# The first eight loads of a one-core gated-mix kernel: who issues them, in what order, and how many warming matmuls stand ahead of them

## The chip, the cores and the metric

The kernel runs on 1 core of one Trainium2 chip. The metric is device time in microseconds of one execution; lower is better. The kernel before took 150.2 us (median of 3 runs, 149.66 to 150.45). A profile is one further execution; its own time and the span of its records are given below.

## What is computed

`x` has 2048 rows of 512 features, all in bf16. Two branches read it and a gate mixes them:

```python
g = sigmoid((x * gate_w).sum(-1))                 # one number per row
# branch a: linear attention with 32 heads of 16 features
q, k, v = split(x @ wqkv)
pq, pk  = q @ w_phi, k @ w_phi                    # per head
phi_q   = concat(softmax(pq), softmax(-pq));  phi_k likewise
kv, z   = sum_s phi_k v,  sum_s phi_k
a = (phi_q kv) / (phi_q z + 1e-6) @ wo
# branch b
b = relu(x @ w1) @ w2                             # w1 is 512 x 1376
out = g * a + (1 - g) * b
```

## The kernel before, in words

Every step is a named task of one engine. Tasks are put down with `add(name, engine, function, deps)`; the table `ORDER` (line 17) fixes by hand in which order each engine runs its tasks, and `settle` (line 133) turns the dependences into semaphore waits in front of a task, leaving out those that another wait already implies. So the order of the work is wholly static: SP issues its DMAs one after the other in the order of `ORDER["sp"]`, ScalarE (ACT) issues its DMAs and its activations in the order of `ORDER["act"]`, and so on. `dur`, `lat` and `boost` are numbers for a planner that is no longer run; they change nothing.

The rows of `x` are taken in four chunks of 512. The matmuls need `x` transposed (`XT`). Chunks 1 to 3 are transposed by DMA (`x1`, `x2`, `x3`). Chunk 0 is wanted first, so it is loaded as it is, in four tiles of 128 rows x 512 features (128 KB each: `x00` to `x03`, issued through `load`, line 306), into a part of `FT` that is free at the start, and TensorE transposes it against an identity matrix.

The front of the kernel, which is all that the change touches, runs like this:

- POOL builds index tiles (`iota_r`, `iota_i`, `iota_c`), then runs two memsets: `ones` (line 283, a column of ones in `VS`) and `hpad`. VectorE (DVE) builds the identity `IDN` (task `ident`, line 354).
- TensorE (PE) first runs `warm0`: six matmuls of 128x512 on a constant, whose result nobody reads (`WARM`, line 218; line 292). They need nothing but the constant.
- Eight loads of 128 KB bring the four tiles of `x` and the first 512 columns of the four row blocks of W1 (`w1a0` to `w1a3`). SP issues `x00 w1a0 w1a2 x02 x03`; ACT issues `x01 w1a1 w1a3`. Behind them SP goes on with `w1b`, `wphi`, `wkT` (a transposing DMA, line 311), `w1c`, `wv` and then `x1`, which waits for `w1c`.
- PE then runs, in this order: `xt00 xt01 xt10 xt11` (two transposing matmuls each, line 384, tiles 0 and 1 of `x`), `hh00 hh01` (four matmuls each, line 439, W1's row block 0 times row tile 0 and row tile 1), `hh1` and `hh2` (four matmuls of 256 columns each, row blocks 1 and 2), `xt20 xt21`, `hh3`, `xt30 xt31`, `hh4` (row block 3), then `hr0 hr1` (line 445) and the rest of the first hidden blocks.
- The transposed tiles leave PSUM by a ScalarE copy (`xe00`, `xe10`, ...; line 396) and a DVE copy (`xe01`, ...; line 399). `hh00` waits for `xe00` and `w1a0`; `hh01` for `xe10`; `hh1` for `w1a1`, `hh2` for `w1a2`, `hh3` for `w1a3`.
- ScalarE's first activation is `xe00`. Its function table has to be loaded before it; that instruction is put ahead of the first activation, behind the three DMAs in ACT's order.

Everything that follows (the hidden layer `h*` at line 425, projections `pr_*` at line 545, `v*` at line 526, the feature maps on ScalarE, DVE and POOL, `kv*`, `nd*`, and the two output matmul groups `b*` at line 676 and `a*` at line 682) is left as it is by the change.

Of the kernel before, what the change touches and what calls it, by code (L numbers as in the profile page):

```python
# [5 lines left out]
ACT = mybir.ActivationFunctionType  # L6
# [9 lines left out]

ORDER = {
# [4 lines left out]
    ),  # L22
# [5 lines left out]
    ),  # L28
    "act": (
# [153 lines left out]
def bass_gated_mix__linear_kernel_hedgehog__dense_activation_relu__prompt_kernel(  # L183
# [11 lines left out]
    x2 = A_x.rearrange("b s d -> (b s) d")  # L195
# [4 lines left out]
    P = 128  # L200
# [14 lines left out]
    NPH, NOM, NOT, NOS = 7, 3, 4, 5  # L215
    NDB, AB = (6, 7), (3, 4, 5, 2)
    GATE_LIMIT = 40.0
    WARM = (6 * (512,),)
    RL = 400.0
    FE = "dve"  # L220

    with ExitStack() as es:
        E = es.enter_context

        def sb(name, shape, dt):
            return E(nc.sbuf_tensor(name, shape, dt))
# [6 lines left out]
        W1 = sb("W1", [P, ND, W1C], BF16)  # L233
# [30 lines left out]
        EP = sb("EP", [P, NT], FP32)  # L264
# [11 lines left out]
        add = g.add  # L276
# [10 lines left out]
        one = nc.const_aps.tensor(1.0, (P, 1), BF16).tensor  # L287
        ones_w, ones_m = (bass.AP(tensor=one, offset=0, ap=[[1, P], [0, n]]) for n in (P, 512))

        def pe_warm(q, cols):  # L290
            for n in cols:
                last = q.matmul(PS[:, 2, 0:n], ones_w, ones_m[:, 0:n], start=True, stop=True)  # L292
            return last

        for n, cols in enumerate(WARM):
            add(f"warm{n}", "pe", lambda q, c=cols: pe_warm(q, c), (), dur=sum(cols) / 1200.0, boost=3000.0)
# [3 lines left out]
        def after_last(name, eng):  # L300
            if eng in queue:
                g.follow(queue[eng], name)
            queue[eng] = name

        def load(name, eng, out_, in_, deps=(), dur=0.1, lat=6.0, **how):
            add(name, eng, lambda q: q.dma_start(out=out_, in_=in_, **how), deps, dur=dur, lat=lat, dma=True,
                boost=1e4)
            after_last(name, eng)
# [9 lines left out]
        w1r = B_w1.rearrange("(j p) n -> p j n", p=P)  # L318
        x0r = x2[chunk(0), :].rearrange("(m p) d -> p m d", p=P)
        wvr = A_wqkv[:, 2 * D:3 * D].rearrange("(j p) n -> p j n", p=P)  # L320
        def load_x(m, eng, lat):
            load(f"x0{m}", eng, XN[:, m, :], x0r[:, m, :], dur=0.45, lat=lat)

        def load_w(j, eng, lat):
            load(f"w1a{j}", eng, W1[:, j, 0:512], w1r[:, j, 0:512], dur=0.45, lat=lat)

        load_x(0, "sp", 2.95)
        load_x(1, "act", 3.1)
        load_w(0, "sp", 3.2)
        load_w(1, "act", 3.4)  # L330
        load_w(2, "sp", 3.8)
        load_w(3, "act", 3.95)
        load_x(2, "sp", 4.0)
        load_x(3, "sp", 3.9)
# [141 lines left out]
        for n, (kind, a, k) in enumerate(units):  # L476
            b = GB4[n] if n < 4 else FB[2] if n == 4 else HB[(n - 4) % len(HB)]
            if kind == "h":
                halved = n < 4
                deps = [*xof[a], *w1of[k], prev, *freed[b]]  # L480
                if k == KT - 1:
# [18 lines left out]
                    deps, dur=(0.22 if k < 2 else 0.44) if halved else 0.87,  # L500
# [5 lines left out]
            else:  # L506
                deps = ["wqT", *wbd, prev, *freed[b]]
# [22 lines left out]
        for m in range(NT):  # L530
            def add(*a, boost=20.0 * (len(widths) * 2 - m // 2 - VLAG), **how):
                return g.add(*a, boost=boost, **how)
# [17 lines left out]
        for jn, (kind, tiles) in enumerate(jobs):  # L550
# [66 lines left out]
            else:  # L617
# [4 lines left out]
                    dur=0.11 + 0.207 * w)  # L622
# [24 lines left out]
                for m in tiles:  # L647
# [39 lines left out]
                    if m == NT - 1:  # L687
# [4 lines left out]
                        for h2 in range(2):  # L692
# [25 lines left out]
                            else:  # L718
                                add(f"oe{m}_1", "dve", lambda q, m=m, b=b, cs=cs: q.tensor_scalar(  # L719
                                    OSB[:, m % NOS, cs], PS[:, b, 0:cs.stop - cs.start], OMG[:, m:m + 1], None, ALU.mult), need,  # L720
                                    dur=0.4)
                            add(f"st{m}_{h2}", ("act", "sp")[h2], lambda q, m=m, cs=cs: q.dma_start(
                                out=o2[m * P:(m + 1) * P, cs], in_=OSB[:, m % NOS, cs]), (f"oe{m}_{h2}",), dur=0.5,
                                lat=1.5, dma=True)
# [55 lines left out]
```

## Time and profile before

| what | us |
|---|---|
| median of 3 runs (lowest, highest) | 150.2 (149.66, 150.45) |
| the profiled execution's own time | 149.87 |
| its span, from its first record to its last | 148.3 |
| PE busy in the span | 145.5 (98%) |
| DVE / POOL / ACT busy | 111.7 / 109.6 / 91.4 |
| moved by DMA | 16.11 MB, 109 GB/s over the span |

The profiled execution took 1.57 us more than its span shows, so 1.57 us lie outside the records. Times in the views count from the span's start. In a row of the timeline the first number is the start, the second how long the (merged) instructions took, then engine, line, operation, the tile written and the one read, the shape and the count; in brackets stands the idle time before it and what ended it. PEld rows are weight loads, which run beside PE's matmuls. SPq and ACTq rows are DMA issues: the time in them is the issuing, not the transfer. Matmuls are pipelined: each row's duration is longer than the distance to the next matmul, so rates are read from starts.

### The profile page before, as it was taken

How to read it: one execution, taken by the hardware profiler on the slowest of the kernel's cores; microseconds unless marked ns; L12 is line 12 of the kernel's file. 1: busy time of each engine (PE TensorE's matmuls, PEld its weight loads, DVE VectorE, ACT ScalarE, POOL GpSimd, SP SyncE). 2: the span in 40 equal slices, each digit the busy share in tenths (PEclk: the TensorE clock that was granted, in tenths of full speed). 3: DMA queues.
4: the chain of work that ended last, by engine and by line, in shares of the span. 5: the costliest groups of instructions: out<-in, count | busy, mean ns of one | idle time of the engine just before them, and what ended most of it. 6: DMA issues, size and time to landing. Idle time of an engine off the chain costs nothing.

```text
span 148.3 us, 2542 instructions
## 1 busy us (share of the span) xinstructions
PE 145.5 (98%) x1009; PEld 75.3 (51%) x1009; DVE 111.7 (75%) x169; ACT 91.4 (62%) x126; POOL 109.6 (74%) x72
## 2 busy tenths in 40 slices
PE   7999999999999999999999999999999999999994
PEld 2875444445654475445444545455444444445453
DVE  2433666998896948989999997999999988634502
ACT  3475769799969765898983937175583751310141
POOL 4000499999999999999999999999999793150000
PEclk9999999999999999999999999999999999999999
DMA  4998999910040001000000093646957785556752
GB/s 139 324 256 220 169 187 214 340 51 4 0 73 0 0 4 38 0 0 4 0 0 0 7 141 71 141 95 138 183 119 167 180 214 116 141 134 158 64 157 92
DMA packets 46363, 16.11 MB, mean 109 GB/s; under 512 B 39856, under 2 KB 46352, under 8 KB 46352
## 3 DMA queue, kind: packets, MB, share of 16 engines
q1 hardware_dynamic: 43760, 13.61, 42.6%
q10 hardware_dynamic: 2592, 2.34, 4.9%
q8 instruction: 8, 0.13, 0.4%
q14 instruction: 3, 0.02, 0.1%
HBM read 4.41 MB, written 2.10 MB: 44 GB/s over the span
## 4 chain that ended last, share of the span: by engine, by line
PE 98%; DVE 0%; issue 0%
PE PS L676 24%; PE PS L425 21%; PE PS L545 19%; PE PS L526 9%; PE PS L682 9%; PE PS L611 3%; PE PS L654 3%; PE PS L433 2%; PE PS L292 2%; PE PS L698 2%; PE PS L439 2%; PE PS L445 1%; PE PS L408 1%; PE PS L384 1%; PE PS L709 1%; DVE OSB L719 0%
## 5 line engine op out<-in xcount | busy, mean ns | idle before, releaser
L590 POOL TENSOR_TENSOR TS<-PB,MX 128x1024 bf16<-128x1024 bf16 (+1 forms) x18 | 30.9, 1723 | 14.5 <-DVE MX L581 14.5
L676 PE MATMUL PS<-W,HT 128*128 128x512 bf16 (+1 forms) x165 | 38.1, 379 | 0.0
L597 DVE TENSOR_REDUCE ZB<-FT 128x128 f32<-128x2048 bf16 (+1 forms) x18 | 36.6, 2031 | 1.8 <-ACT FT L595 1.8
L595 ACT ACTIVATE FT<-TS 128x2048 bf16<-128x2048 bf16 (+1 forms) x18 | 30.9, 1718 | 9.6 <-POOL TS L590 9.5
L425 PE MATMUL PS<-XT,W 128*128 128x512 bf16 x144 | 34.7, 379 | 0.0
L590 POOL TENSOR_TENSOR TS<-MN,PB 128x1024 bf16<-128x1024 bf16 (+1 forms) x18 | 30.9, 1726 | 0.8 <-DVE MN L583 0.8
L545 PE MATMUL PS<-WP,XT 128*128 128x512 bf16 x128 | 30.6, 379 | 0.0
L604 POOL TENSOR_TENSOR FT<-FT,SC 128x2048 bf16<-128x2048 bf16 (+1 forms) x9 | 29.6, 3293 | 0.0
L503 ACT ACTIVATE HT<-PS 128x512 bf16<-128x512 f32 x40 | 22.6, 597 | 5.4 <-PE PS L425 4.6
L581 DVE TENSOR_REDUCE MX<-PB 128x64 bf16<-128x1024 bf16 (+1 forms) x18 | 19.5, 1085 | 5.9 <-ACT PB L577 5.9
L676 PEld LDWEIGHTS PS<-W,HT 128*128 128x128 bf16 (+1 forms) x165 | 15.4, 98 | 16.9
L730 ACT ACTIVATE OSB<-PS,OMG 128x512 bf16<-128x512 f32 x14 | 9.6, 686 | 21.1 <-PE PS L682 20.5
L583 DVE TENSOR_REDUCE MN<-PB 128x64 bf16<-128x1024 bf16 (+1 forms) x18 | 19.3, 1084 | 3.2 <-ACT PB L577 3.2
L425 PEld LDWEIGHTS PS<-XT,W 128*128 128x128 bf16 x144 | 13.7, 98 | 15.4
L577 ACT ACTIVATE PB<-PS 128x1024 bf16<-128x1024 f32 (+1 forms) x18 | 16.7, 927 | 7.2 <-PE PS L545 4.0
L545 PEld LDWEIGHTS PS<-WP,XT 128*128 128x128 bf16 x128 | 12.1, 98 | 13.5
L526 PE MATMUL PS<-WV,XT 128*128 128x512 bf16 x64 | 16.4, 379 | 0.0
L627 POOL TENSOR_TENSOR FT<-FT,SR 128x1024 bf16<-128x1024 bf16 (+1 forms) x9 | 15.7, 1740 | 0.7
L682 PE MATMUL PS<-WO,OT 128*128 128x512 bf16 x60 | 14.9, 378 | 0.0
L663 DVE SCALAR_TENSOR_TENSOR OTM<-PS,EG,RD 128x256 bf16<-128x256 f32 x32 | 13.8, 463 | 0.2
L661 DVE RECIPROCAL RD<-PS 128x16 f32<-128x16 f32 x32 | 6.4, 232 | 9.0 <-PE PS L654 8.8
L535 ACT ACTIVATE VS<-PS 128x512 bf16<-128x512 f32 x16 | 9.6, 602 | 4.3 <-PE PS L526 4.3
(55 smaller groups left out, 106.6 us busy)
## 6 DMA issues: line engine op xcount, KB each, us to landing
out_dram<-OSB ACTq DMA_DIRECT2D x14, 128.0 KB, 2.2
W<-in_B_w_dram SPq DMA_DIRECT2D x1, 1280.0 KB, 7.5
W<-in_B_w_dram SPq DMA_DIRECT2D x1, 512.0 KB, 4.5
WV<-in_A_wqkv_dram SPq DMA_DIRECT2D x1, 512.0 KB, 4.9
WO<-in_A_wo_dram SPq DMA_DIRECT2D x1, 512.0 KB, 7.5
FT<-in_A_x_dram SPq DMA_DIRECT2D x3, 128.0 KB, 3.1
W<-in_B_w_dram SPq DMA_DIRECT2D x1, 352.0 KB, 4.1
W<-in_B_w_dram ACTq DMA_DIRECT2D x2, 128.0 KB, 3.3
```

Of the source, the lines that this page charges most:

```text
L425: last = q.matmul(PS[:, b, :], W1[:, j, k * P:(k + 1) * P], XT[:, j, chunk(c)], start=(j == 0), stop=(j == ND - 1))
L503: add(f"rl{a}_{k}", "act", lambda q, a=a, k=k, b=b: q.activation(HT[:, k, chunk(a)], PS[:, b, :], ACT.Relu), (prev,), dur=0.6, boost=RL)
L526: last = q.matmul(PS[:, 2, :], XT[:, j, m * P:(m + 1) * P], WV[:, j, :], start=(j == 0), stop=(j == ND - 1))
L545: last = q.matmul(PS[:, n, :], XT[:, j, m * P:(m + 1) * P], WP[:, s, j, :], start=(j == 0), stop=(j == ND - 1))
L581: add(f"mx_{J}", "dve", lambda q, sl=sl, w=w, i=pbg: q.tensor_reduce(MX[:, sl, 0:w * H], i, AX.X, ALU.max), (f"ev_{J}", old("t1")), dur=0. ...
L583: add(f"mn_{J}", "dve", lambda q, sl=sl, w=w, i=pbg: q.tensor_reduce(MN[:, sl, 0:w * H], i, AX.X, ALU.min), (f"ev_{J}", old("t2")), dur=0. ...
L590: add(f"{tn}_{J}", "pool", lambda q, o3=o3, a3=a3, b3=b3: q.tensor_tensor(o3, a3, b3, ALU.subtract), (f"{'mx' if sg == 0 else 'mn'}_{J}", ...
L595: add(f"ex_{J}", "act", lambda q, fs=fs, ts=ts, w=w: q.activation(FT[:, fs, 0:w * F], TS[:, ts, 0:w * F], ACT.Exp), (f"t1_{J}", f"t2_{J}", ...
L597: add(f"sm_{J}", "dve", lambda q, fs=fs, sl=sl, w=w: q.tensor_reduce(ZB[:, sl, 0:2 * w * H], FT[:, fs, 0:w * F].rearrange("p (g d) -> p g ...
L604: add(f"nm_{J}", "pool", lambda q, f3=f3, sl=sl, w=w: q.tensor_tensor(f3, f3, SC[:, sl, 0:2 * w * H].unsqueeze(2).to_broadcast([P, 2 * w * ...
L676: last = q.matmul(PS[:, ab, :], HT[0:r, k, m * P:(m + 1) * P], W2[0:r, k, :], start=(k == 0), stop=False)
L682: last = q.matmul(PS[:, ab, :], OT[:, m % NOT, t, :], WO[:, t, :], start=False, stop=(t == ND - 1))
```

## The change

```diff
 ORDER = {
     "sp": (
-        "x00 w1a0 w1a2 x02 x03 w1b wphi wkT w1c wv x1 x2 wqT x3 gw w2a w2b wo hx0 hx1 hx2 tq0 tq1 "
+        "x00 x01 w1a0 w1a1 x02 x03 w1b wphi wkT w1c wv x1 x2 wqT x3 gw w2a w2b wo hx0 hx1 hx2 tq0 tq1 "
...
     "act": (
-        "x01 w1a1 w1a3 xe00 xe10 xe20 xe30 rl0_0 rl0_1 rl0_3 rl0_2 rl0_4 fe1_1 fe1_3 rl0_5 ev_k0 rl0_8 rl0_6 "
+        "first w1a2 w1a3 xe00 xe10 xe20 xe30 rl0_0 rl0_1 rl0_3 rl0_2 rl0_4 fe1_1 fe1_3 rl0_5 ev_k0 rl0_8 rl0_6 "
...
-    WARM = (6 * (512,),)
+    WARM = (5 * (512,),)
...
-        def load_w(j, eng, lat):
-            load(f"w1a{j}", eng, W1[:, j, 0:512], w1r[:, j, 0:512], dur=0.45, lat=lat)
+        def load_w(j, eng, lat, deps=()):
+            load(f"w1a{j}", eng, W1[:, j, 0:512], w1r[:, j, 0:512], deps, dur=0.45, lat=lat)
 
         load_x(0, "sp", 2.95)
-        load_x(1, "act", 3.1)
+        load_x(1, "sp", 3.1)
         load_w(0, "sp", 3.2)
-        load_w(1, "act", 3.4)
-        load_w(2, "sp", 3.8)
+        load_w(1, "sp", 3.4)
+        add("first", "act", lambda q: q.activation(EP[:, 0:1], bass.AP(tensor=one, offset=0, ap=[[1, P], [1, 1]]), ACT.Copy),
+            (), dur=1.5)
+        after_last("first", "act")
+        load_w(2, "act", 3.8, ("ones",))
         load_w(3, "act", 3.95)
```

SP now issues six of the eight first loads, `x00 x01 w1a0 w1a1 x02 x03`, one more than before. ACT issues two, `w1a2` and `w1a3`, and the first of them waits until POOL's memset `ones` is done. Ahead of both stands a new activation, `first`, which copies one constant per partition into a column of `EP` that is overwritten much later; the function table is now loaded ahead of it. One of the six warming matmuls is taken away. Nothing else moves.

## The prediction

> **What bounds the kernel now.** I read the page first, sections 1 and 4: who is busy, and what the chain that ended last is made of.
>
> ```profile
> span 148.3 us, 2542 instructions
> ...
> PE 145.5 (98%) x1009; PEld 75.3 (51%) x1009; DVE 111.7 (75%) x169; ACT 91.4 (62%) x126; POOL 109.6 (74%) x72
> ...
> PE 98%; DVE 0%; issue 0%
> ```
>
> The chain is PE alone. The waits of PE over the whole span have one row:
>
> ```profile
> PE PS L292 <- PEq L765: 0.8, 1, 0.8
> ```
>
> That is the start, before the first warming matmul. Behind it PE waits for nobody long enough to be listed, so the kernel lasts as long as PE's list of matmuls, counted from when PE can begin it. Only three things can move the end: when the real matmuls begin, how fast they run, and a hole that a late load tears. So the timeline of the first microseconds comes next (shown in part).
>
> ```profile
> 0.74 0.41 ACTq L306 DMA_DIRECT2D FT<-in_A_x_dram  x1
> 0.74 0.40 SPq L306 DMA_DIRECT2D FT<-in_A_x_dram  x1
> ...
> 0.77 2.72 PE L292 MATMUL PS<-const-bfloat16-1.0 128*128 128x512 bf16 x6 [0.77 <-PEq L765]
> ...
> 1.42 0.67 POOL L283 MEMSET VS<- 128x128 bf16 x1
> ...
> 2.15 1.28 ACT L396 ACT_TABLE_LOAD   x1 [2.15 <-issue]
> ...
> 3.55 0.78 PEld L384 LDWEIGHTS PS<-IDN,FT 128*128 128x128 bf16 x8 [0.96 <-issue]
> ...
> 3.58 1.01 PE L384 MATMUL PS<-IDN,FT 128*128 128x128 bf16 x8
> 3.99 0.81 ACT L396 ACTIVATE XT<-PS 128x256 bf16<-128x256 f32 x2 [0.56 <-PE PS L384]
> ...
> 4.43 1.98 PE L439 MATMUL PS<-XT,W 128*128 128x128 bf16 x16
> 6.14 0.32 PEld L384 LDWEIGHTS PS<-IDN,FT 128*128 128x128 bf16 x4
> 6.24 0.39 PE L384 MATMUL PS<-IDN,FT 128*128 128x128 bf16 x4
> ...
> 6.47 0.38 PE L439 MATMUL PS<-XT,W 128*128 128x256 bf16 x2
> ```
>
> Three readings. First, real work begins at 3.58 and x00 sets that: the DMA view of the two issues at 0.74 gives
>
> ```profile
> FT<-in_A_x_dram ACTq DMA_DIRECT2D x1, 128.0 KB, 2.9
> FT<-in_A_x_dram SPq DMA_DIRECT2D x1, 128.0 KB, 2.7
> ```
>
> so x00 lands at 3.45 (0.13 before the first transpose) and x01 at 3.64. Second, the rate. Eight transposes take 4.43 - 3.58 = 0.85 us, 106 ns each; four later ones take 6.47 - 6.24 = 0.23, 57 ns each. PE starts at half rate and changes over, though the granted clock on the page is full throughout. When: the 16 matmuls between 4.43 and 6.24 are 8 of 128 columns and 8 of 256, which is 8 x 0.107 + 8 x 0.213 = 2.56 us at half rate and 1.32 us at full (0.056 and 0.109). They took 1.81. With t at half rate, t + (2.56 - t) x 0.516 = 1.81 gives t = 1.01: the change-over is at about 5.44, which is 4.67 us after the first warming matmul. Third, the warming matmuls start 0.43 apart, so the sixth has run out at about 3.3, and PE stands 0.29 until 3.58.
>
> **The change part by part.** *x00 alone.* The table by stretches shows how the transfers fill the DMA engines:
>
> ```profile
> 1.70:2.30 0.60, 0.60 (x3) 0.18 (x2) 0.60 (x1) 0.15 (x1) 0.59 (x2) 1.00 0.41 41
> 2.30:5.10 2.80, 2.71 (x18) 1.52 (x17) 0.92 (x3) 1.90 (x3) 0.00 (x0) 1.00 1.04 363
> ```
>
> (last columns: granted clock, DMA share, GB/s). From 2.30 to 5.10 they are full at 363 GB/s. Before 2.30 only 41 GB/s x 0.6 us = 25 KB came, which I give to x00. The other 106 KB of x00 run beside as much of x01: 212 KB at 363 are 0.58 us; alone, 0.29. So x00 lands 0.29 sooner, at 3.16, and the first transpose starts at 3.29. Bounds: 0 if the first transfer's latency is fixed, and 0.36 (128 KB at 363) if x01 stood wholly ahead of it; I take 0.29, from the bytes.
>
> The Trainium skill, "DMA: Bandwidth & Descriptors", section "Issuing engines are not separate DMA queues", says that transfers from several issuers share the same DMA engines and that a second issuer saves only issue time. The full stretch above agrees; by it the saved issue time is what the change gives up, which is rival B below.
>
> *Five warming matmuls.* One of 0.43 us goes. The sixth would run out at 3.3, just when x00 now allows the start, so taking it away is worth nothing if x00 lands at 3.16 and up to 0.14 if it lands earlier; it is what makes an earlier start possible. PE then stands from 2.87 to 3.29, 0.42 us in place of 0.29.
>
> *What 0.29 us is worth.* It lies ahead of the change-over. If that stays at 5.44, PE does 0.29 us more of half-rate work before it, which at full rate would be 0.29 x 0.516 = **0.15 us**. Were the change-over ahead of 3.29, all 0.29 would count.
>
> *x01, w1a0, w1a1 in line on SP.* SP's issues stand 0.46 to 0.47 apart, 0.40 to 0.43 of it the instruction. Issues become x01 1.20 (was 0.74), w1a0 1.66 (was 1.20), w1a1 2.13 (was 1.18 on ACT). The quickest load seen takes 2.71 us from issue to landing beside another; 2.42 alone, by the sum above. With 2.42 they land at 3.62, 4.08 and 4.55. PE wants x01 at 3.29 + 4 x 0.107 = 3.72, w1a0 at 4.14, w1a1 at 5.00 (8 matmuls of 0.107 later). All fit, the first two by 0.1 or less. Upper end: x00's shared 2.71 for x01 and w1a0's own 2.9 for w1a0, landing at 3.91 and 4.56: that is rival B.
>
> *ScalarE.* `first` brings the table load (1.28 us) from 2.15 to about 0.74, ending at 2.02, plus one tiny copy: no such row, so between 0 and the 0.38 of a 128x256 copy; I take 0.2, nearer the small end. ACT is idle then, so this is free. xe00 now wants the table at about 3.70 (3.99 less 0.29); at 2.15 + 1.28 = 3.43 it would have been ready anyway. The new wait on `ones` ends at 1.42 + 0.67 = 2.09. Behind it in ACT's order stand w1a2, w1a3 and xe00. w1a2 is issued at 2.15 to 2.40 (was 1.66), w1a3 0.46 later. With 2.42 to 3.2 us they land at 4.6 to 5.6 and 5.0 to 6.1; PE wants them at 5.66 and about 6.3. xe00 has over a microsecond to spare.
>
> *SP's queue behind it.* SP issues one load more than before, so x02 (2.13, now 2.60), x03 (2.60, now 3.08) and all behind them, w1b, wphi, wkT, w1c, wv and x1, are issued 0.47 later. Landings by the rows, issue plus time to landing, moved by 0.47, against first use moved by 0.15: x02 2.60 + 3.2 = 5.8 against 6.1; x03 6.2 against 6.5; w1b 8.1 against 8.85; wkT 10.0 against 10.6 (line 408 begins at 10.73); x1, which waits for w1c, 17.7 against 18.4 (h1_0 is the second half of the eight matmuls at 17.66). wphi, w1c and wv have more. So 0.47 costs nothing; another 0.3 would begin to.
>
> **Sum.** 149.87 - 0.15 = 149.72 for an execution like the profiled one, which lay 0.33 under the median shown. On that median: 150.2 - 0.15 = 150.05; I say 150.0.
>
> **The rivals.** *B: a load comes too late.* If w1a0 lands at 4.56 as its own 2.9 says, hh00 starts at about 4.60 where it was 4.43: 0.17 us at half rate, 0.09 lost: 150.3. For it: it is third on SP's queue instead of second. Against: fewer bytes stand ahead of it or beside it.
>
> *C (slower): the longer stand resets PE's rate.* If whatever raises the rate counts again after a stand of between 0.29 and 0.42 us, the 4.67 us run from 3.29 to 7.96, 2.52 us later; at half rate that loses 2.52 x 0.484 = 1.22, less the 0.15: 151.3. For it: the sixth matmul covered just this time. Against: the present stand of 0.29 did no such thing. If x00 does not land sooner either, the stand is 0.72, so C grows likelier with a small gain.
>
> The Trainium skill, "TensorE: Matmul & The Clock Gate", Part 1, has the rate rise only after a busy window of about 3.4 us, one of a fixed grid that does not start with the kernel. The change-over at 5.44 fits such a window begun at 2.03, in which PE stood 0.29; no run here shows the grid. By it a window that the longer stand spoils costs an estimated 1.7 us, and the time would be 151.75; and runs differ by where the grid falls.
>
> *D (faster): the change-over comes sooner.* Every 1 us by which it moves is worth 0.48. The three runs lie 0.79 apart, which is 1.6 us of it if that is their cause. With a change-over 1.2 us sooner than in the median run and 0.29 fully counted: 150.2 - 0.58 - 0.29 = 149.3. For it: the spread. Against: nothing in the change starts PE sooner; it would be chance.
>
> *E: the change does not do what it says:* x00 lands at 3.45 as before since the first bytes set it; then 150.2.
>
> **Chances.** Forecast 0.50 (150.05), E 0.12 (150.2), B 0.13 (150.3), C 0.11 (151.3), D 0.14 (149.3). What one measurement of this kernel can tell from no change is about 0.5%, 0.75 us. So slower 0.12 (C, and a tail of B), faster 0.15 (D, and a tail of the forecast), same 0.73. The range reaches from D to past B: 149.3 to 150.9; it leaves out C and half of D, under 0.2.
>
> **What would show it.** Right: the first transpose (line 384) at about 3.3, PE's stand before it 0.4, hh00 (line 439) at about 4.14, the change-over near 5.4, PE still alone on the chain. E: first transpose at 3.5 or later. B: a stand ahead of line 439 near 4.1 to 4.6. C: matmuls of 128 columns still 107 ns apart after 6.3. Wrong altogether: a new wait of PE beyond 8 us, on wkT or x1.

## The result, and the profile after

The changed kernel is slower by half a per cent: 151.12 us in the median of 22 runs (149.83 to 152.34), against 150.31 (149.57 to 150.74) for the kernel before in as many. The ratio is 1.0053 with a 95% interval of 1.0028 to 1.0078: small, but clear of the noise. The forecast was 150.0 with a range to 150.9, so the time lies outside. Not only the median moved: the spread grew from 1.2 us to 2.5. The times form two groups of 11 with nothing between 150.89 and 151.34, and the median stands in that gap. The execution of 152.34 counts as slow, being over 1.5% above the quickest, and without it the median would be 150.89. Below, the executions of 151.2 us or more are called the upper group.

The profiled execution took 150.69 us, 0.82 more than the one of before, with 1.6 us outside its span. Its page, sections 1 and 4:

```profile
span 149.1 us, 2541 instructions
...
PE 91%; DMA 5%; SPq 2%; issue 0%; DVE 0%
```

PE is busy 145.4 us, as before (145.5). The chain is no longer PE alone: 5% of it is a DMA and 2% SP's queue, which is 10 us. The waits of PE say where the chain leaves PE:

```profile
PE PS L292 <- PEq L768: 0.8, 1, 0.8
PE PS L442 <- DMA W<-in_B_w_dram: 0.6, 1, 0.6
PE PS L411 <- DMA WT<-in_A_wqkv_dram: 0.4, 1, 0.4
```

The first row was there before; the other two are new. PE waits for a block of W1 ahead of line 442 (439 before: the hidden products), and for `wkT` ahead of the fold at line 411 (408 before), the matmuls that multiply `wkT` by w_phi. The timeline of the first microseconds puts times to them (start, length, engine, line; in brackets the idle time ahead and what ended it):

```profile
3.02 1.08 PE L387 MATMUL PS<-IDN,FT 128*128 128x128 bf16 x8
3.92 1.05 PE L442 MATMUL PS<-XT,W 128*128 128x128 bf16 x8
4.57 4.64 SPq L311 DMA_TRANSPOSE WT<-in_A_wqkv_dram  x1
...
5.57 1.05 PE L442 MATMUL PS<-XT,W 128*128 128x256 bf16 x8 [0.61 <-DMA W<-in_B_w_dram]
6.46 0.39 PE L387 MATMUL PS<-IDN,FT 128*128 128x128 bf16 x4
...
9.26 1.90 PE L428 MATMUL PS<-XT,W 128*128 128x512 bf16 x8
11.52 1.05 PE L411 MATMUL PS<-WBD,WT 128*128 128x128 bf16 x16 [0.36 <-DMA WT<-in_A_wqkv_dram]
```

Read it against the timeline of before. The first transpose starts at 3.02 where it was 3.58: 0.56 us gained, more than forecast. hh00 starts at 3.92 (was 4.43). The eight 128-column products behind it last 0.85 us at half rate, so PE is through at 4.77 and stands 0.80 us until hh1 at 5.57 (the bracket says 0.61, because the end of a matmul is modelled). By the next transposes, 6.46 against 6.24, the gain has become a loss of 0.22. Line 428 starts at 9.26 (line 425: 9.00). The eight of it needed 1.73 us before; here the fold starts 2.26 behind their start, so 0.53 us more are lost. The fold begins at 11.52 against 10.73, which is 0.79 of the 0.82 us. From there to the end both kernels take the same: 139.17 and 139.14 us.

The loads that PE waits for, by the DMA view of the two issues at 2.12 (last number: us from issue to landing):

```profile
W<-in_B_w_dram ACTq DMA_DIRECT2D x1, 128.0 KB, 3.2
W<-in_B_w_dram SPq DMA_DIRECT2D x1, 128.0 KB, 3.4
```

The second is w1a1: landed at 5.53, just ahead of hh1. The first is w1a2, landed at 5.30. The chain of waits, in order of time (start, length), shows the other one:

```profile
4.57 6.81 DMA WT<-in_A_wqkv_dram
11.39 0.14 issue
11.52 1.05 PE PS L411 x16
```

`wkT` was issued at 4.57, 0.47 later than before as forecast, but took 6.81 us to land, where the prediction had taken 5.4 from the profile of before. Ahead of it in SP's queue stand the 16 KB of `wphi` and, ahead of these, `w1b`, the 512 KB load issued at 3.55. Its row on the page of before, then of after (last number: us from issue to landing):

```profile
W<-in_B_w_dram SPq DMA_DIRECT2D x1, 512.0 KB, 4.5
```
```profile
W<-in_B_w_dram SPq DMA_DIRECT2D x1, 512.0 KB, 5.7
```

So `w1b` landed at 9.21 where it was 7.56. The stretch from 2.30 to 5.10 (last columns: granted clock, DMA share, GB/s; a packet's time and bytes are both counted in the stretch in which it starts):

```profile
2.30:5.10 2.80, 2.67 (x18) 1.41 (x16) 0.92 (x3) 0.77 (x2) 0.00 (x0) 1.00 0.93 261
```

The DMA engines are nearly as full as in the same stretch of before (0.93, was 1.04) but move 261 GB/s, not 363. A later stretch shows more:

```profile
8.70:9.20 0.50, 0.50 (x7) 0.36 (x4) 0.00 (x0) 0.50 (x2) 0.00 (x0) 1.00 0.08 15
9.30:9.80 0.50, 0.50 (x4) 0.26 (x4) 0.17 (x1) 0.49 (x2) 0.00 (x0) 1.00 1.26 281
```

Right before `w1b` is through, at 9.21, hardly anything starts to move; right behind it 281 GB/s do. That is `wkT` held up and then let go. In the trace 21 of its 256-byte packets take 0.58 to 1.56 us, where 18 ns is the rule, and all of them end between 9.25 and 9.29.

### The profile page after: what moved, and what is told of

Same layout as the page of the kernel before. It is cut to its first block, busy times and chain, and to the rows that moved or that the text cites. A ratio compares the mean times of both kernels' runs of the same rounds, so it can differ in the third digit from the quotient of the medians.

```text
span 149.1 us, 2541 instructions
## 1 busy us (share of the span) xinstructions
PE 145.4 (98%) x1008; PEld 74.8 (50%) x1008; DVE 111.7 (75%) x169; ACT 91.6 (61%) x127; POOL 109.6 (73%) x72
## 4 chain that ended last, share of the span: by engine, by line
PE 91%; DMA 5%; SPq 2%; issue 0%; DVE 0%
PE PS L679 24%; PE PS L428 20%; PE PS L548 19%; PE PS L529 9%; PE PS L685 9%; DMA WT<-in_A_wqkv_dram 5%; PE PS L614 3%; PE PS L657 3%; SPq L306 2%; PE PS L436 2%; PE PS L701 2%; PE PS L411 1%; PE PS L712 1%; DVE OSB L722 0%
```

## The experiments

Four theories stood at the start. **Meeting queues**: ACT's loads, issued behind SP's, slow the transfers where the two queues join. **Line**: six issues one after the other on one queue leave the DMA engines less full than two queues do. **Hole and rate**: a longer stand of PE in the first microseconds makes its change to the full rate come late in some executions, which gives the upper half of the spread. **wkT**: the 0.47 us by which SP's later loads move stands directly on the path.

**Which part of the change.** All six loads on one queue (e1); the sixth warming matmul put back (e2); w1a2 without its wait (e3); ACT's queue used once, early, for a 4 KB load into a buffer that nothing reads (e4).

```diff
 e1: after, with
-        "x00 x01 w1a0 w1a1 x02 x03
+        "x00 x01 w1a0 w1a1 w1a2 w1a3 x02 x03
-        "first w1a2 w1a3 xe00
+        "first xe00
 e2: after, with
-    WARM = (5 * (512,),)
+    WARM = (6 * (512,),)
 e3: after, with
-        load_w(2, "act", 3.8, ("ones",))
+        load_w(2, "act", 3.8)
 e4: after, with
-        "first w1a2 w1a3 xe00
+        "touch first w1a2 w1a3 xe00
+        load("touch", "act", DUM[:, :], x0r[:, 0, 0:DH])
```

> The two loads of ACT go to SP behind w1a1 (x00 x01 w1a0 w1a1 w1a2 w1a3 x02 x03); ACT only runs the new first activation. Theory 'meeting queues' (the DMA engines slow down when ACT's queue joins SP's at 3.1 to 4.1 us, and everything behind is late): the slow stretch near 3.5 is gone, w1a1 lands near 4.4 instead of 5.53, PE has no hole ahead of line 439's first 256-column matmul; what is left is SP's longer line (x02 on are 0.9 us later than in the changed kernel), which may cost up to 0.4 at x02 or at wkT. Total 149.6 to 150.4. Theory 'SP's line' (w1a1 is late because it is fourth to be issued): w1a1 lands at 5.3 or later, the hole of 0.6 to 0.9 us stays, total 151 or more. Theory 'rate' (the longer stand of PE delays the change-over): 151, with 128-column matmuls 107 ns apart beyond 6.3 us.

> The changed kernel with six warming matmuls again. 'Meeting queues' and 'SP's line': the first transpose moves from 3.02 to about 3.35, the hole ahead of line 439's 256-column matmuls shrinks by as much and takes it up; total within 0.2 of the changed kernel (150.9 to 151.3). 'Rate': the stand is gone, and the total comes back to 150.0 to 150.3.

> The changed kernel, but w1a2 does not wait for the memset: ACT issues w1a2 and w1a3 as soon as its sequencer reaches them. If the table load does not hold the issue back, they go out at 0.75 and 1.2, the two queues meet at the very start, x00 lands at about 3.4 as before, w1a1 near 4.5: 'meeting queues' gives no hole at line 439 and a total of 150.0 to 150.4. If the table load holds it back, w1a2 goes out at 2.05 and nothing changes: 151. 'SP's line': w1a1 stays late (5.3), hole stays, 151.

> The changed kernel with a 4 KB load on ACT's queue at 0.74, whose data nobody reads, ahead of the first activation. If the slow stretch belongs to the first use of ACT's queue, it moves to about 2.1 us (x00 lands at 3.1 to 3.4 instead of 2.89), the stretch at 3.5 is gone, w1a1 lands near 4.5, no hole, total 149.8 to 150.3. If it belongs to ACT's loads joining loads in flight, whichever is first, it stays at 3.3 to 4.1 and the total stays near 151. 'SP's line': also 151.

| kernel | median us (range, runs) | ratio to before (95%) |
|---|---|---|
| e1, one queue | 151.12 (150.49 to 151.36, 10) | 1.0061 (1.0039 to 1.0083) |
| e2, six warming | 150.44 (150.25 to 150.69, 12) | 1.0015 (1.0001 to 1.003) |
| e3, no wait for `ones` | 151.15 (150.25 to 152.64, 12) | 1.0059 (1.0028 to 1.0091) |
| e4, early touch | 150.8 (149.96 to 152.29, 12) | 1.0034 (1.0005 to 1.0062) |

e1 speaks against the meeting of queues: with one queue only, nothing joins, and the loads as a whole are no sooner. w1a1 does land at 4.39, as that theory expected, but then nothing lands until w1a2 at 5.58 (in the changed kernel, nothing between 3.78 and 5.30), and the last of the eight lands at 6.61 against 6.39. A stretch of it (same columns), and two rows of PE's waits:

```profile
4.70:5.30 0.60, 0.48 (x5) 0.18 (x2) 0.00 (x0) 0.00 (x0) 0.00 (x0) 1.00 0.99 229
```
```profile
PE PS L442 <- DMA W<-in_B_w_dram: 0.7, 2, 0.5
PE PS L428 <- DMA W<-in_B_w_dram: 0.6, 1, 0.6
```

The DMA share is 0.99 at 229 GB/s, and PE now waits for blocks of W1 three times, once at line 428 for w1b. `wkT` is issued at 5.52, 0.95 later than in the changed kernel, lands at 11.96, and the fold starts at 12.10: the profiled time is 151.24. That is the price of two more places in SP's queue. e4 speaks against the meeting of queues too: the slow stretch stays (155 GB/s between 3.5 and 4.1).

e3 shows nothing gained by dropping the wait. w1a2 is issued at 0.80 instead of 2.12 and the time stays at 151.15. ACT's two W1 blocks then stand beside x00 and x01; x00 itself comes later (PE waits 0.3 us for it and starts at 3.34), and w1a0 lands at 4.60, where it landed at 3.78 in the changed kernel.

e2 is the clearest answer: with one more warming matmul the median is 0.68 us lower, and the spread falls from 2.5 us to 0.44. No execution of 12 is at 151.2 or above; of the 34 of e1, e3 and e4, measured beside it with five warming matmuls, 14 are. Its loads are little better than those of the changed kernel: `wkT` lands at 10.94, and PE, not `wkT`, sets the start of the fold (11.30). So what it removes seems to pass through PE. PE in its profile:

```profile
3.29 1.06 PE L387 MATMUL PS<-IDN,FT 128*128 128x128 bf16 x8
...
5.52 1.45 PE L442 MATMUL PS<-XT,W 128*128 128x256 bf16 x8 [0.31 <-DMA W<-in_B_w_dram]
```

It starts real work 0.27 later than the changed kernel and gets to hh1 at the same time: the load w1a1 sets hh1, and the earlier start only bought a longer stand.

**Line against rate.** The kernel before with its second load held back 0.36 us by waiting for a small POOL result (e5), which staggers the issues but keeps both queues; the changed kernel with idle matmuls in the hole ahead of hh1 (e6); the kernel before with five warming matmuls (e7); the changed kernel once more (e8, nothing edited).

```diff
 e5: before, with
-        load_x(1, "act", 3.1)
+        load_x(1, "act", 3.1, ("iota_r",))
 e6: after, with
-    hh00 hh01 hh1
+    hh00 hh01 warm1 hh1
+        def pe_fill(q):
+            for _ in range(4):
+                last = q.matmul(PS[:, 0, 256:512], ones_w, ones_m[:, 0:256], start=True, stop=True)
+            return last
+        add("warm1", "pe", pe_fill)
 e7: before, with
-    WARM = (6 * (512,),)
+    WARM = (5 * (512,),)
```

> The kernel before, with one edit: ACT's first load (x01) waits for POOL's first iota, so that ACT's three loads start about 0.35 us later than SP's; both queues stay in use and hold loads ahead of the DMA engines. If the changed kernel's late loads come from feeding the engines from one line of issues 0.47 us apart ('line': the engines run dry and out of step), they stay full here after 2.4 us, x00 lands at 2.9 to 3.2, w1a1 by 4.7, w1b by 7.8, wkT by 9.7, PE has no hole: 149.9 to 150.3, ratio 0.998 to 1.0. If a second queue that joins a running one is what slows them ('meeting queues'), the slow stretch appears at about 2.5 to 3, w1a1 lands beyond 5 and wkT beyond 10.3: 150.5 to 151.

> The changed kernel, with four idle matmuls of 256 columns (0.85 us at half rate, into PSUM columns that nobody reads) between hh01 and hh1, that is, in the hole in which PE waits for w1a1. They bring no load earlier. If the upper half of the changed kernel's times (151.3 to 152.3) are executions in which the hole spoils PE's rise to full rate, these go away: median 150.3 to 150.7, spread under 0.8 us. If the loads alone make those times, the fill changes nothing or costs: 151.1 and a spread of 2 us or more.

> The kernel before with five warming matmuls; the loads are as before. PE then stands from 2.87 to 3.58, 0.7 us, with no hole later. If a stand of 0.7 us within the first 4 us is enough to delay the rise to full rate in part of the executions, the times split, with an upper group 1.2 to 1.7 us above the lower one: median 150.5 to 151.2. If not, same as before: 150.0 to 150.4.

> The changed kernel once more, for a second profile. Its times fall into 149.8 to 150.9 and 151.3 to 152.3. If this execution falls into the upper group and PE's rate is the cause, matmuls of 256 columns run at 0.213 us beyond 5.6 us, up to about 8 or 9; if the loads are the cause, they run at 0.109 and the waits on w1b and wkT are longer by over 1 us.

e5 took 150.17 (149.82 to 150.33, 12 runs; ratio 1.0, 0.9982 to 1.0017), as the line theory expected. Its loads are later than that theory expected, though (`w1b` at 8.46, not 7.8), and a stretch of it is slow:

```profile
7.70:8.90 1.20, 1.20 (x16) 1.11 (x15) 0.09 (x1) 0.95 (x2) 0.00 (x0) 1.00 0.81 122
```

With two queues the loads can be late as well: `wkT` lands at 10.63, 6.5 us after its issue. So a late `wkT` does not need the single line of issues. Whether the line adds to it is taken up at the end of the next section.

e6 took 150.59 (150.14 to 151.06, 12 runs; 1.0027, 1.0007 to 1.0047). In its profile the four idle matmuls start at 5.16 and hh1 behind them at 5.70. In that execution w1a1 had landed at 5.05, so there was no stand left there to fill. No execution reached 151.2, which agrees with the sixth warming matmul; with the changed kernel's later executions beside it (3 of 20, below) it would not show anything by itself. e7 took 150.41 (149.98 to 151.64, 12 runs; 1.0021, 0.9997 to 1.0045): not told apart from no change, with one execution at 151.64. e8 took 150.49 in its one execution, `wkT` landing at 11.20.

**Was the profile of before typical?** A copy of the kernel before (e9, nothing edited), the changed kernel with three warming matmuls (e10), and the kernel before with `first` ahead of ACT's loads, x01 behind `iota_r` and five warming matmuls (e11), which has the early table load and x00 alone in front, but leaves the loads on their two queues.

```diff
 e10: after, with
-    WARM = (5 * (512,),)
+    WARM = (3 * (512,),)
 e11: before, with
-    WARM = (6 * (512,),)
+    WARM = (5 * (512,),)
-        "x01 w1a1 w1a3 xe00
+        "first x01 w1a1 w1a3 xe00
-        load_x(1, "act", 3.1)
+        add("first", "act", ...)
+        load_x(1, "act", 3.1, ("iota_r",))
```

> The kernel before once more, for a second profile. If the DMA stretch of the first profile (2.3 to 5.1 us at 363 GB/s, wkT landing at 9.5) is what this order of loads always gives, it comes again: w1a2 at 4.8, wkT at 9.3 to 9.7. If the first profile was a lucky execution, as the loads of the kernel before with five warming matmuls suggest, wkT lands at 10.2 to 10.8 and w1a2 at 5.2 to 5.7, and about 0.9 us of the lateness of wkT in the changed kernel is not the change's.

> The changed kernel with three warming matmuls instead of five. Loads are the same, and PE cannot begin x00's transposes sooner than 3.0 us, so a theory of late loads alone gives the changed kernel's times again (median 151.1, both groups). If PE's rate rises only after a stretch in which PE was busy enough, the stand from 2.0 to 3.0 makes the late group the rule: median 151.6 to 152.1, few or none under 150.9, and in the profile 256-column matmuls at 0.213 us beyond 6 us.

> The loads of the kernel before on both queues, but ACT's three wait for the first iota (0.35 us), the table load stands ahead of them, and there are five warming matmuls: x00 lands at 2.85, PE's first transpose is at 3.0, and w1a1 and w1a2 are issued 0.6 and 0.5 us sooner than in the changed kernel. If holes at hh1 are what spoils the changed kernel, this gives 149.8 to 150.1 with a spread under 1.3; if the five warming matmuls alone spoil it, 150.4 or more.

e9 took 150.52, and its profile changes the reading of all that came before. The same stretch of the first profile of before, then of e9, which is the same kernel:

```profile
7.70:8.90 1.20, 1.20 (x19) 1.12 (x17) 1.08 (x7) 0.80 (x2) 0.00 (x0) 1.00 1.33 270
```
```profile
7.70:8.90 1.20, 1.20 (x21) 1.09 (x19) 0.70 (x3) 0.48 (x2) 0.00 (x0) 1.00 0.27 47
```

Between 7.7 and 8.9 us e9 moves 47 GB/s where the first moved 270. Its `wkT` lands at 10.88, 6.79 us after issue, against 9.46 and 5.35 in the first. x03 is late as well: it lands at 7.29, and PE waits for it. The first profile, from which every landing in the prediction was read, was the luckiest of all in the landing of `wkT`, and the unluckiest in that of x00 (3.45, the latest of all).

e10 shows a late change of rate in a trace:

```profile
6.71 0.63 PE L387 MATMUL PS<-IDN,FT 128*128 128x128 bf16 x4
7.14 0.64 PE L442 MATMUL PS<-XT,W 128*128 128x256 bf16 x2
7.64 0.61 PE L387 MATMUL PS<-IDN,FT 128*128 128x128 bf16 x4
...
11.90 1.06 PE L411 MATMUL PS<-WBD,WT 128*128 128x128 bf16 x16
```

Four transposes take 7.14 - 6.71 = 0.43 us, 107 ns each, and four more from 7.64 are hardly quicker; PE is at half rate until a little past 8. In the changed kernel's profile the four at 6.46 took 0.22. Here PE, not `wkT` (which lands at 11.11), sets the fold at 11.90, and the profiled time is 151.05. The late change of rate is what "hole and rate" expected of this trace. The median is 151.08 (150.61 to 151.46, 6 runs; 1.0056, 1.0034 to 1.0078), below what it expected, and two of the six are at 151.2 or above.

e11 took 150.21 (149.37 to 151.87, 12 runs; 0.9994, 0.9974 to 1.0015). The median is that of before, but two of 12 executions are at 151.2 or above, and the quickest is at 149.37. Neither expectation fits: the spread of 2.5 us is too wide for the one, the median too low for the other.

**The sixth matmul with the old loads, and more profiles.** e11 with six warming matmuls (e14), and five more copies of the changed kernel (e12, e13, e15, e16, e17, nothing edited), to catch an execution of the upper half with a profile and to see which load sets the time.

```diff
 e14: e11, with
-    WARM = (5 * (512,),)
+    WARM = (6 * (512,),)
```

> The changed kernel, a third profile. An execution of the upper group (151.3 and more), if it is one: 'hole and rate' wants 256-column matmuls at 0.213 us beyond 6 us and the change-over at 7 to 9; 'late loads alone' wants the change-over before 6 and waits on w1b and wkT that are over 1 us longer than in the lower group. An execution of the lower group: change-over by 5.7.

> The changed kernel, a fourth profile, for the same question: upper group with a change-over at 7 to 9 by 'hole and rate', upper group with a change-over before 6 and waits over 1 us longer by 'late loads alone'.

> The kernel with both queues 0.36 us apart and the table load first, with six warming matmuls in place of five; nothing else differs. PE's first transpose goes from 3.01 to 3.29. 'Hole and rate' (starting earlier only lengthens the wait for the later loads, and the wait delays the change-over in some executions): the times over 151 go away, median 149.9 to 150.2, spread under 0.9. 'Loads alone': the spread of 2.5 us stays, and the median is 0 to 0.15 above that of five.

> The changed kernel, a fifth profile, for one execution of the upper group (14 of its 39 times so far are 151.2 or more). Upper group by 'hole and rate': change-over at 7 to 9. By 'late loads alone': change-over before 6, and waits on W1's later columns and wkT over 1 us longer.

> The changed kernel, a sixth profile, the same question and the same numbers.

> The changed kernel, a last profile. In all six so far the fold (line 411) begins 0.14 us after wkT lands, and the execution's time is that start plus 139.16. If this one is under 151.2, the same: time is wkT's landing plus 139.30. If it is 151.2 or more: by 'hole and rate' wkT lands by 11.7 as before, the fold begins over 0.3 us behind it, and the change-over is at 7 to 9; by 'late loads alone' the fold still begins 0.14 behind wkT, which lands at 11.9 or later.

e14 took 150.06 (149.52 to 150.37, 12 runs; 1.001, 0.9993 to 1.0028): with the sixth warming matmul no execution is high, and the spread goes from 2.5 us to 0.85. It is not told apart from before, and no version here is faster than before. The copies: e12 150.5 (149.97 to 151.24, 8 runs; 1.0036, 1.0012 to 1.0059), e13 150.65 (149.83 to 151.47, 8 runs; 1.0053, 1.0028 to 1.0077), and 150.96, 150.17 and 150.16 in one execution each of e15, e16 and e17. With e8 that makes seven profiles of one kernel:

| profile | w1b lands | wkT lands | fold starts | time of that execution |
|---|---|---|---|---|
| after | 9.21 | 11.39 | 11.52 | 150.69 |
| e8 | 9.02 | 11.20 | 11.34 | 150.49 |
| e12 | 8.93 | 11.11 | 11.24 | 150.38 |
| e13 | 8.36 | 10.54 | 10.68 | 149.83 |
| e15 | 9.47 | 11.64 | 11.78 | 150.96 |
| e16 | 8.71 | 10.88 | 11.01 | 150.17 |
| e17 | 8.70 | 10.86 | 10.99 | 150.16 |

In each the fold starts 0.13 to 0.14 us behind the landing, and the time is the start of the fold plus 139.14 to 139.18. e17 came out as was expected of it: 10.86 + 139.30 = 150.16. So in all seven, `wkT` sets the time; by the starts of the matmuls ahead of the fold, PE waited for it 0.02 to 0.53 us, 0.34 on average. And `wkT` in turn follows `w1b`: in all seven it lands 2.16 to 2.18 us behind it.

None of the seven profiles fell among the upper group, which is thinner here: 3 of the 20 executions of these copies reach 151.2 us, against 11 of the first 22.

## Why the prediction was wrong

**The step that failed: "wkT 10.0 against 10.6 ... So 0.47 costs nothing".** The mechanism was named ("another 0.3 would begin to", and a wait on `wkT` was called what would be "wrong altogether"); the size was off. The 10.0 came from one execution, in which the load took 5.4 us. Over six profiles with SP's old order (before, e5, e7, e9, e11, e14) it takes 5.35, 6.5, 6.2, 6.8, 5.9 and 6.4, mean 6.2; over the seven of the changed kernel 6.0 to 7.1, mean 6.5. So the landing moved not by 0.47 but by 0.79 on average, from 10.30 to 11.09. The 0.6 us of slack that the forecast had left over was never there on average: two of those six (e5, e14) were already bound by `wkT`, at 10.63 and 10.47. So the later issue on SP went on the path.

The forecast counted `wkT`'s time from its issue. The traces tie it to the load ahead: in 18 of the 19 profiles it lands 2.0 to 2.2 us behind `w1b` (1.9 in the first of before), and its long packets end within 0.13 us of `w1b`'s landing. So whatever makes `w1b` late reaches the fold too, and `w1b`, issued 0.47 later, lands 0.72 later on average (8.91, was 8.19). What holds the packets is not shown.

How much it costs: the seven profiled executions average 150.38 us, against a median of 150.16 over the 132 executions of the kernel before. That gives an estimate of 0.2 us. e12 and e13, measured beside a kernel before of 150.01, are 0.5 and 0.6 us slower with only three of 16 executions in the upper group.

**"2.42 us from issue to landing" for the first four loads of SP.** It held for the first two (x00 landed 2.15 us after its issue, x01 2.25); the third, w1a0, took 2.1 to 2.9 in the seven profiles. It failed for the fourth: w1a1 took 3.41 and landed at 5.53, where PE wanted it at 5.00. The sum took the DMA engines to run at 363 GB/s; in the changed kernel they moved 261. Rival B ("a load comes too late") did happen. In three of the seven profiles (e8, e12, e16) it happened as it was written: w1a0 landed at 4.37, 4.09 and 4.56, and PE stood 0.5 to 0.9 us ahead of hh00. In all seven it also stood one load further on, ahead of hh1, 0.2 to 0.9 us.

**x00 alone, 0.29 sooner.** Right in kind: x00 landed at 2.78 to 2.91 in the seven profiles. Against the 3.45 of the first profile of before that is 0.5 to 0.7 us sooner, against e9 (3.13) and e7 (3.26), whose first loads are those of before, 0.2 to 0.5. So the size came out about right, but from a landing of x00 that was late itself. Rival E fell. But the 0.15 us that an earlier start was to bring never reached the end, since w1a1 set when hh1 could run; and with six warming matmuls, which begin real work 0.27 later, hh1 starts at the same time (5.52 against 5.57).

**"Taking it away is worth nothing".** This is the second failed step, and the larger one: the removal of the sixth warming matmul was put into the sum at nothing, and rival C, a price for it, at a chance of 0.11. Three pairs of versions differ in that matmul alone. Two of them set the two orders of loads side by side (in e11 and e14 ACT's first load also waits for the first iota, and `first` stands ahead of it):

| loads, warming matmuls | median us | kernel before, beside it | 151.2 us or more |
|---|---|---|---|
| old order, six (e14) | 150.06 | 150.01 | 0 of 12 |
| old order, five (e11) | 150.21 | 150.19 | 2 of 12 |
| new order, six (e2) | 150.44 | 150.19 | 0 of 12 |
| new order, five (the changed kernel) | 151.12 | 150.31 | 11 of 22 |

So neither part makes the 0.8 us alone: the new order costs 0.25 with six warming matmuls, five cost nothing in the median with the old order, and together they bring the upper group. (The third pair, e7 and before, has 150.41 and 150.16, not told apart.)

All executions of 151.2 us or more, with five warming matmuls: 14 of 42 of the changed kernel with its copies, 4 of 10 of e1, 6 of 12 of e3, 4 of 12 of e4, 2 of 12 of e11, 1 of 12 of e7. With three, 2 of 6 (e10). With six, none of 12 in e2, e5 and e14, and 2 of 132 of the kernel before. The fill of e6 has 0 of 12. The rows of the table were not all measured together, and the share of the upper group in the changed kernel itself went from 11 of 22 to 3 of 20. But e2 was measured together with e1, e3 and e4: 0 of 12 against 14 of 34. The upper 14 have a median of 151.7, the lower 28 one of 150.4.

**Is the upper part rival C, a rate that rises late?** Not by the stand that C named: ahead of the first transpose PE stood only 0.05 to 0.19 us in the seven profiles, not 0.42; the long stands lie ahead of hh00 and hh1. For a late rate in another way: what removes the upper group acts on PE alone and does not bring the loads sooner. `wkT` would have to land at about 12.4 for 151.7 us (151.7 - 139.16 - 0.13), 7.8 us after issue, where 7.1 was the longest of all; and in e2 it comes no sooner than otherwise. The change-over was found at very different times, too: at 5.5 in before, between 3.6 and 5.6 in the profiles of the changed kernel, at 6.4 in e2, 6.7 in e7 and past 8 in e10. The Trainium skill, "TensorE: Matmul & The Clock Gate", Part 1, has the rate rise on a fixed grid that does not start with the kernel, so that the same start can meet it early or late; this scatter agrees with it. Seven of the traces also hold entries of the granted clock. Full clock begins there at 5.48 us in before, 5.37 in e5, 5.83 in e9, 5.89 in e11, 6.38 in e2, 6.72 in e7 and 3.78 in e1, and lasts 143.36 us in six of them and 146.77 in e1: 42 and 43 times 3.413 us, as steps of a fixed length would give.

Against it, or open: no profile of an upper execution of the changed kernel was caught, so no trace of it shows a late rise at 151.7 us. The one profiled execution above 151.2, that of e1 (151.24), has its full clock early and is late by `wkT`, at 11.96. In e4's profile PE stood from 3.82 to 5.12 and ran at full rate behind it (150.29), so a long stand does not always bring a late rate. And e10, which has the late rate, began its fold at 11.90, while 151.7 us needs 12.5. How late the rate rises in an upper execution, and whether a late load is added to it, stays open. That the upper group comes almost only with a warming matmul missing, and mostly with the new order of loads, is what the runs show; that the rate is the way it comes about is the likelier reading, not shown.

**What also stays open** is why the loads of one kernel land so differently. Between 2.30 and 5.10 us the DMA engines moved 363 GB/s in the first profile of before, 292 to 321 in the five others with the old order of loads, 255 to 275 in the seven of the changed kernel and 244 in e1 with all on one queue, at shares of 0.86 to 1.04. So the order of issues does tell, and the theory of the line is not disposed of: e5 and e9 show only that `wkT` can also land late with two queues. The scatter between executions of one kernel comes on top, and its cause is not shown. The meeting of two queues is not needed for it (e1).

## What to carry to other kernels

Read slack from several profiles of the same kernel, not from one: the landing of a load near the path moved by 1.4 us between two executions, and a slack of 0.6 was luck. A load added to an issue queue moves everything behind it, and the price stands at the load with the least slack, far from the edit. Look also at what a load waits for on the DMA engines: here `wkT` came when the load ahead of it was through, not a fixed time after its own issue. A stretch of warming matmuls is to be sized against the first wait that remains: starting real work sooner was worth nothing here, where the next load was late, and taking a warming matmul away cost more than it was to bring.

## What the runs showed of the hardware

The same 512 x 512 transposing load took 5.35 to 7.1 us from issue to landing. In these traces it was held on the DMA engines until the load ahead of it was through. In this stretch of the changed kernel the DMA share is 1.69 at only 93 GB/s:

```profile
7.70:8.90 1.20, 1.20 (x21) 1.14 (x19) 0.33 (x3) 0.58 (x2) 0.00 (x0) 1.00 1.69 93
```

The share is that high because it counts the whole time of the held 256-byte packets, up to 1.56 us each, which start here. So a high share is not work done. Packets of 1 KB, 46 ns as a rule, took up to 1.23 us in that trace as well, before this stretch.

A table load did not hold back the DMA issues of its own engine. In e3 ACT loads its table from 0.73 to 2.01, and its two loads of W1 are issued from 0.80 on:

```profile
0.73 1.28 ACT L331 ACT_TABLE_LOAD   x1 [0.73 <-PEq L768]
0.80 0.88 ACTq L306 DMA_DIRECT2D W<-in_B_w_dram  x2
```

The granted clock reads 1.00 in every stretch shown, those at half rate too. In the trace of before the first entry of the clock is the one at 5.48 us, so ahead of it the 1.00 rests on no entry; there the rate of PE has to be read from how far apart matmuls of one shape start (107 ns and 56 ns for 128 columns).
